# Gate and value of a gated MLP by Strassen's seven products, in three passes over the features

## The chip, the core and the metric

One NeuronCore of a Trainium2 chip runs the whole program in one launch. The metric is the device time of one execution in microseconds (us). Times of one kernel are medians over several runs; the profile is one profiled execution.

## The reference

An attention over chunks feeds two MLPs, all in float32 with 3072 tokens and a model width of 512. The change touches the second MLP alone:

```python
def _moe2_ref(x, w_gate, w_val, w_out):      # x 3072x512, w_gate, w_val 512x1536, w_out 1536x512
    g = x @ w_gate
    silu = g * (1.0 / (1.0 + np.exp(-g)))
    val = x @ w_val
    return (silu * val @ w_out).astype(np.float32)
```

Its input x is the output of the first MLP (width 2048, squared ReLU). The weights arrive as 64-bit floats and are turned into float32 on the chip.

## The kernel before, in words

Precision: every float32 operand of a large matmul is split into a rounded part `hi` and a residue `lo` (both float32r), and a product is three matmuls into one PSUM bank, hi*hi, hi*lo and lo*hi (`product`, L417 to 420). A weight tile and its rounding are made by `split` (L591): ScalarE or VectorE takes the magnitude of the upper words, VectorE bounds (L606), shifts (L610), sets sign and lower bits (L615, L622), one of the two rounds to `hi`, and VectorE subtracts (L632).

Staging: the first MLP goes over eight tiles of 384 tokens; each tile's output is stored to `y_dram`. The second MLP goes over the same eight tiles. For each tile t and each of the 12 feature tiles j of 128 features (a step), TensorE makes `gate` and `val` (`second_up`, L529: four blocks of k of 128, three matmuls of 384 columns each, so 12 and 12), ScalarE takes silu of gate (L542), VectorE multiplies by val (L546), one of the two rounds the product to `ghi`, VectorE makes the residue `glo` (L478), and in the step after TensorE adds three 128-token pieces of the down product, nine matmuls of 512 columns, to the accumulators `oacc` (`second_down`, L548). After twelve steps the accumulators are copied out (L558) and stored to `out`. All 36 weight tiles of the second MLP are converted once, in 18 pairs of 1 MB, and stay in SBUF; the memory for them comes from slots of `wp` (17, each held by one converted pair or one raw pair) that the first MLP's last tile gives back one by one, and two more (`EXTRA`).

Order: no engine chooses its work at run time. `Plan` (its `run`) is a list scheduler in the program: each piece of work has an engine, an assumed length, dependencies, and buffers as counted rooms (`get`, `put`) or rings (`take`, `give`). TensorE's order is the order in which pieces are added; the order on VectorE, ScalarE and SyncE (which issues all DMAs) is that in which the planner's clock would start them, the longest way to the end first. Each engine then runs its instructions in that order and waits on semaphores. `either` picks ScalarE or VectorE for a piece, by the list `MOVED`.

The step's order on TensorE in the second MLP stands in the loop at L861: `plan_up2` of a step, then `plan_down2` of the step before.

Of the kernel before, what the change touches and what calls it, by code (L numbers as in the profile page):

```python
# [14 lines left out]
ALU = mybir.AluOpType  # L15
# [118 lines left out]
def attention_and_two_mlps(  # L134
# [41 lines left out]
    N2 = 3 * M2 // 2  # L176
    EXTRA = 2
# [30 lines left out]
    part_dram = dram.tile([P, KD, T], F32, name="part_dram")  # L208

# [39 lines left out]
    def source2(i):  # L249
        j, n = divmod(i, 3)  # L250
        cols = slice(j * P, (j + 1) * P)
        return (w_gate[:, cols], w_val[:, cols], w_out2[cols, :])[n]

    def load_w2(p):
        raw2[p] = load_slot((source2(2 * p), source2(2 * p + 1)), f"second{p}")

    def weight2(j, n):
        p, h = divmod(3 * j + n, 2)
        w = w2[p]
        return w[:, 0, h * 512:(h + 1) * 512], w[:, 1, h * 512:(h + 1) * 512]  # L260
# [156 lines left out]
    def product(o, whi, wlo, xhi, xlo, first, last):  # L417
        nc.tensor.matmul(o, whi, xhi, start=first, stop=False)  # L418
        nc.tensor.matmul(o, whi, xlo, start=False, stop=False)  # L419
        nc.tensor.matmul(o, wlo, xhi, start=False, stop=last)  # L420
# [89 lines left out]
    yp = w2p = None  # L510
    y_f = {}

    def load_y(t, i):
        yf = yp.tile([P, T], F32, tag="yf", name=f"yf{t}_{i}")
        nc.sync.dma_start(out=yf, in_=y_dram[t][:, i])
        y_f[t, i] = yf

    def round_y(engine, t, i):
        if i == 0:
            y_t[t] = tuple(xp.tile([P, KD, T], F32R, tag=f"x{n}", name=f"y{n}{t}") for n in ("hi", "lo"))  # L520
        copy(engine, y_t[t][0][:, i], y_f[t, i])

    def residue_y(t, i):
        yhi, ylo = y_t[t]
        nc.vector.tensor_tensor(
            out=ylo[:, i], in0=y_f.pop((t, i)), in1=yhi[:, i].bitcast(F32), op=ALU.subtract
        )

    def second_up(t, j, n):  # L529
        yhi, ylo = y_t[t]  # L530
        pool, tag = ((ps_h, "h"), (ps_a, "a"))[n]
        o = pool.tile([P, 512], F32, tag=tag, name=("gate", "val")[n])[:, :T]
        whi, wlo = weight2(j, n)
        for kd in range(KD):
            c = slice(kd * P, (kd + 1) * P)
            product(o, whi[:, c], wlo[:, c], yhi[:, kd, :], ylo[:, kd, :], kd == 0, kd == KD - 1)
        g_t[t, j, n] = o

    def second_silu(t, j):
        r = gp.tile([P, T], F32, tag="r", name="sil")  # L540
        g_t[t, j] = r, None
        nc.scalar.activation(out=r, in_=g_t.pop((t, j, 0)), func=AF.Silu)  # L542

    def second_times(t, j):
        r, _ = g_t[t, j]
        nc.vector.tensor_tensor(out=r, in0=g_t.pop((t, j, 1)), in1=r, op=ALU.mult)  # L546

    def second_down(t, j, i):  # L548
        whi, wlo = weight2(j, 2)
        phi, plo = g_t[t, j]  # L550
        if j == 0:
            acc[t, i] = ps_acc.tile([P, 512], F32, tag=f"acc{i}", name=f"oacc{i}")
        c = slice(i * P, (i + 1) * P)
        product(acc[t, i][:, :DM], phi[:, c], plo[:, c], whi, wlo, j == 0, j == M2 - 1)

    o_t = {}

    def second_out(engine, t, i):  # L558
        o = o_t[t, i] = yp.tile([P, DM], F32, tag="o", name="o", bufs=2)
        copy(engine, o, acc[t, i][:, :DM])  # L560

    def second_store(t, i):
        r0 = t * T + i * P
        nc.sync.dma_start(out=out[r0:r0 + P, :], in_=o_t.pop((t, i)))
# [5 lines left out]
        dict(w=SLOTS - LENT, fly=2),  # L570
        dict(
            sc=LENT, f=2, own=1, q=2, k=2, v=3, kt=2, qt=1, at=1, x=2, r=3, ghi=2, glo=2, acc01=1,
            acc23=1, a=2, h=2, yf=3, o=2,
# [17 lines left out]
    def split(landed, raw, key, pool, name, done):  # L591
# [33 lines left out]

        def hi(engine):
            done[key] = pool().tile([P, 2, CH], F32R, tag="w", name=f"w_{name}")
            copy(engine, done[key][:, 0], held["f"].bitcast(F32))
# [13 lines left out]
        t = plan.add(DVE, 1.14, rest, [t], lag=0.5)  # L642
        t = either(f"h_{name}", {ACT: 0.95, DVE: 0.65}, hi, [t], lag=0.5)
        return plan.add(DVE, 1.14, lo, [t], put=["w"])
# [109 lines left out]
    y_parts = {}  # L754

    def open_second():
        nonlocal w2p, yp
        attn.close()
        w2p = ctx.enter_context(tc.tile_pool(name="w2p", bufs=EXTRA, reuse_waits="tile"))
        yp = ctx.enter_context(tc.tile_pool(name="yp", bufs=3, reuse_waits="tile"))  # L760

    def plan_w2(p):
        if p not in split2:
            landed = transfer(opened, lambda: load_w2(p), 2, 1024, ["w"] if p < EXTRA else ["w", "w"])
            split2[p] = split(landed, raw2, p, lambda: w2p if p < EXTRA else wp, f"second{p}", w2)
        return split2[p]

    def plan_y(t):
        y_parts[t] = []
        for i in range(KD):  # L770
            y = transfer([*opened, y_stored[t, i]], lambda i=i: load_y(t, i), 1, 192, take=["yf"])
            hi = either(f"z{t}_{i}", {ACT: 0.45, DVE: 0.35}, lambda e, i=i: round_y(e, t, i), [y, *y_parts[t][-1:]], take=["x"] if i == 0 else ())
            y_parts[t].append(plan.add(DVE, 0.48, lambda i=i: residue_y(t, i), [hi], give=["yf"]))

    def plan_up2(t, j):
        gate = plan.add(
            PE, 2.08, lambda: second_up(t, j, 0), [plan_w2(3 * j // 2), *y_parts[t]], take=["h"]
        )
        e = plan.add(ACT, 0.50, lambda: second_silu(t, j), [gate], take=["r"], give=["h"])
        val = plan.add(  # L780
            PE, 2.08, lambda: second_up(t, j, 1), [plan_w2((3 * j + 1) // 2)], take=["a"],
            give=["x"] if j == M2 - 1 else (),
        )
        e = plan.add(DVE, 0.57, lambda: second_times(t, j), [val, e], give=["a"])
        e = either(f"p{t}_{j}", {ACT: 0.43, DVE: 0.35}, lambda e: round_hi(e, t, j), [e], take=["ghi"])
        g_ready[t, j] = plan.add(DVE, 0.48, lambda: residue(DVE, t, j), [e], take=["glo"], give=["r"])

    def plan_down2(t, j):
        outs = []
        for i in range(NSUB):  # L790
            outs.append(plan.add(
                PE, 2.08 / NSUB, lambda i=i: second_down(t, j, i),
                [g_ready[t, j], plan_w2((3 * j + 2) // 2), *(acc_free[i:i + 1] if j == 0 else ())],
                give=["ghi", "glo"] if i == NSUB - 1 else (),
            ))
        if j == M2 - 1:
            for i in range(NSUB):
# [50 lines left out]
    for s in range(len(order) + 1):  # L848
        for half in range(2):
# [7 lines left out]
            if half and s > downs:  # L857
                plan_down1(*order[s - 1])
    opened.append(plan.add(SP, 0.1, open_second, [last_x[0]]))
    plan_y(0)  # L860
    for s in range(NB * M2 + 1):  # L861
        if s < NB * M2:
            t, j = divmod(s, M2)
# [45 lines left out]
```

## Time and profile before

| | |
|---|---|
| median of 3 runs | 1293.04 us (1291.48 to 1293.15) |
| profiled execution, first to last instruction (span) | 1292.1 us |
| TensorE matmul busy | 1261.9 us, 7776 matmuls |
| VectorE busy | 590.1 us |
| ScalarE busy | 504.4 us |
| mean granted TensorE clock | 0.996 |

The profile records one execution. PE is TensorE's matmul, PEld its weight load, DVE VectorE, ACT ScalarE, SPq the queue of DMAs that SyncE issues. Matmuls overlap in the pipeline and their ends are modelled, so how fast they follow each other is read from the start times, not from the durations. L542 is line 542 of the kernel. A row `a<-b` names what an instruction writes and reads.

### The profile page before, as it was taken

Reading aid. Unit: us, or ns where it says so; the run is one execution under the profiler, and the core shown is the slowest. Engines: PE = TensorE matmul, PEld = TensorE weight load, DVE = VectorE, ACT = ScalarE, POOL = GpSimd, SP = SyncE. Lnnn points to the kernel's source line nnn. Section 1 sums busy time; section 2 is a strip of 40 time slices with the busy share of each in tenths; the row PEclk is TensorE's granted clock in tenths of the full one; section 3 lists DMA queues with packets and bytes.
Section 4 is the critical chain, followed back from the end, with each engine's and each line's share of the span. In section 5 each row is a group of like instructions: output and inputs, shape, how many; then the busy total and the mean of one; then the engine's idle time right before and its main releaser. Section 6 shows DMA issues by size and latency. Waiting matters only on the chain.

```text
span 1292.1 us, 19275 instructions
## 1 busy us (share of the span) xinstructions
PE 1261.9 (98%) x7776; PEld 1200.1 (93%) x7776; DVE 590.1 (46%) x1406; ACT 504.4 (39%) x1248; POOL 0.7 (0%) x6
## 2 busy tenths in 40 slices
PE   5899999999999999999999999999999999999998
PEld 4788999999999999999999999999999999999997
DVE  6999765444444444453999841211212121121211
ACT  6976555545445454442565221211212121121111
POOL 0000000000000000000000000000000000000000
PEclk9899999999999999999999999999999999999999
DMA  9972232112121121110663210000101000000000
GB/s 191 263 211 97 74 83 70 39 38 62 32 62 38 39 62 32 48 48 13 214 226 123 89 51 1 25 25 1 50 1 49 1 28 22 1 31 1 25 1 25
DMA packets 131201, 80.42 MB, mean 62 GB/s; under 512 B 95144, under 2 KB 124328, under 8 KB 131112
## 3 DMA queue, kind: packets, MB, share of 16 engines
q1 hardware_dynamic: 131112, 79.19, 22.6%
q8 instruction: 61, 1.00, 0.3%
q14 instruction: 28, 0.23, 0.1%
HBM read 65.80 MB, written 13.37 MB: 61 GB/s over the span
## 4 chain that ended last, share of the span: by engine, by line
PE 92%; DVE 4%; ACT 3%; issue 1%; DMA 1%; SPq 0%; ACTq 0%; DVEq 0%
PE hp L418 7%; PE acc L419 6%; PE acc L418 6%; PE acc L420 6%; PE hp L419 6%; PE hp L420 6%; PE gate L420 5%; PE gate L418 5%; PE gate L419 5%; PE oacc L419 5%; PE oacc L420 5%; PE val L420 5%; PE val L418 5%; PE val L419 5%; PE oacc L418 5%; PE psS L329 3%
## 5 line engine op out<-in xcount | busy, mean ns | idle before, releaser
L546 DVE TENSOR_TENSOR sil<-val,sil 128x384 f32<-128x384 f32 x96 | 53.5, 557 | 362.0 <-PE val L420 362.0
L418 PE MATMUL hp<-xhi,w_first 128*128 128x384 f32 x512 | 177.7, 347 | 0.0
L419 PE MATMUL acc<-glo,w_first 128*128 128x384 f32 x512 | 171.6, 335 | 2.9 <-DVE glo L478 2.7
L418 PE MATMUL acc<-ghi,w_first 128*128 128x384 f32 x512 | 172.2, 336 | 1.6 <-ACT kq L212 1.3
L420 PE MATMUL acc<-ghi,w_first 128*128 128x384 f32 x512 | 171.4, 335 | 0.0
L419 PE MATMUL hp<-xlo,w_first 128*128 128x384 f32 x512 | 171.4, 335 | 0.0
L420 PE MATMUL hp<-xhi,w_first 128*128 128x384 f32 x512 | 171.3, 335 | 0.1
L542 ACT ACTIVATE sil<-gate 128x384 f32<-128x384 f32 x96 | 47.2, 492 | 265.8 <-PE gate L420 265.7
L420 PE MATMUL gate<-yhi,w_second 128*128 128x384 f32 x384 | 129.5, 337 | 0.0
L418 PE MATMUL gate<-yhi,w_second 128*128 128x384 f32 x384 | 129.3, 337 | 0.0
L419 PE MATMUL gate<-ylo,w_second 128*128 128x384 f32 x384 | 129.0, 336 | 0.0
L418 PE MATMUL val<-yhi,w_second 128*128 128x384 f32 x384 | 128.3, 334 | 0.0
L419 PE MATMUL val<-ylo,w_second 128*128 128x384 f32 x384 | 128.3, 334 | 0.0
L420 PE MATMUL val<-yhi,w_second 128*128 128x384 f32 x384 | 128.3, 334 | 0.0
L458 DVE SCALAR_TENSOR_TENSOR r<-r,s_sb 128x384 f32<-128x384 f32 x99 | 61.0, 616 | 141.1 <-ACT r L447 141.0
L420 PE MATMUL oacc<-w_second,glo 128*128 128x512 f32 x288 | 114.0, 396 | 0.0
L419 PE MATMUL oacc<-w_second,ghi 128*128 128x512 f32 x288 | 113.7, 395 | 0.0
L212 ACT ACTIVATE ghi<-sil 128x384 fp32r<-128x384 f32 x89 | 46.8, 526 | 167.4 <-DVE sil L546 166.6
L418 PE MATMUL oacc<-w_second,ghi 128*128 128x512 f32 x288 | 111.9, 389 | 0.0
L362 ACT ACTIVATE sc<-sc,mx 96x128 f32<-96x128 f32 x256 | 99.3, 392 | 22.6 <-DVE mx L357 22.4
L447 ACT ACTIVATE r<-hp 128x384 f32<-128x384 f32 x116 | 56.8, 489 | 124.9 <-PE hp L420 124.0
L419 PEld LDWEIGHTS acc<-glo,w_first 128*128 128x128 f32 x512 | 96.1, 188 | 4.2 <-DVE glo L478 3.6
(103 smaller groups left out, 2164.1 us busy)
## 6 DMA issues: line engine op xcount, KB each, us to landing
raw_first<-in_moe_w_in_dram SPq DMA_DIRECT2D x16, 512.0 KB
raw_first<-in_moe_w_out_dram SPq DMA_DIRECT2D x16, 512.0 KB
q<-in_q_dram SPq DMA_DIRECT2D x32, 192.0 KB
y_dram<-y SPq DMA_DIRECT2D x32, 192.0 KB
raw_second<-in_moe_w_gate_dram SPq DMA_DIRECT2D x12, 512.0 KB
raw_second<-in_moe_w_val_dram SPq DMA_DIRECT2D x12, 512.0 KB
yf<-y_dram SPq DMA_DIRECT2D x32, 192.0 KB
raw_second<-in_moe_w_out_dram SPq DMA_DIRECT2D x12, 512.0 KB
```

The costliest lines, as they stand in the source:

```text
L212: nc.scalar.activation(out=out, in_=in_, func=AF.Copy)
L329: nc.tensor.matmul(banks[e][:GQ, j * GK:(j + 1) * GK], qt[r, j, :], kt[r, j, :], start=True, stop=True)
L362: nc.scalar.activation(out=sc[:, h, :], in_=sc[:, h, :], func=AF.Exp, bias=mx[:, h:h + 1], scale=SCALE, accum_out=sm[:, h:h + 1],)
L418: nc.tensor.matmul(o, whi, xhi, start=first, stop=False)
L419: nc.tensor.matmul(o, whi, xlo, start=False, stop=False)
L420: nc.tensor.matmul(o, wlo, xhi, start=False, stop=last)
L447: nc.scalar.activation(out=r, in_=hp, func=AF.Relu)
L458: nc.vector.scalar_tensor_tensor(out=r, in0=r, scalar=s_sb[:, 0:1], in1=r, op0=ALU.mult, op1=ALU.mult)
L542: nc.scalar.activation(out=r, in_=g_t.pop((t, j, 0)), func=AF.Silu)
L546: nc.vector.tensor_tensor(out=r, in0=g_t.pop((t, j, 1)), in1=r, op=ALU.mult)
```

## The change

The second MLP is rearranged.

- Tiles of 512 tokens (`TS`), six of them (`NS`), each seen as two halves of 256 tokens (`TH`). The model width of 512 is seen as two halves of 256, and gate and value of one feature tile as the two halves of the output. On this 2x2 by 2x2 block product Strassen's scheme with seven products (Winograd's form) replaces the eight block products. A product has two k blocks of 128 and three split terms: six matmuls of 256 columns.
- The operand sums are made by VectorE: on the weights in `block_sum` (four sums of 256 columns for a feature tile, in the raw tile), on the tokens in `y_sums` (four of 512 elements). `hi` and `lo` of seven weight blocks take two slots for one feature tile; the down weights of two feature tiles take one slot.
- The output sums use two PSUM banks a step. Chain A takes product 1, is copied (`second_keep`, ScalarE), takes product 6 on top, is copied, takes 7, is copied, takes 4: that is the gate of the first half. Chain B takes 2 (VectorE adds the first copy: value of the first half), is begun anew with 5 (plus the third copy: gate of the second half) and takes 3 on top (plus the second copy: value of the second half).
- silu, product, rounding and residue are done by halves of 256 tokens. The down product takes four pieces of 128 tokens.
- Three passes (`PASSES`) of four feature tiles (`JP`), each over all six token tiles. The accumulators hold a pass; its sum is stored to `sum_dram`, loaded again in the next pass and added by VectorE. The seven token operands are made in the first pass, stored to `ops_dram` and loaded again in the other two.
- A pass's weights are loaded while the pass before runs, as slots come free (`put` at the last tile).

The core of the diff; the loop at its end sets TensorE's order:

```diff
+    TS = 512
+    TH = TS // 2
+    NS = NT // TS
+    PASSES = 3
+    JP = M2 // PASSES
...
+    def second_up(n, op):
+
+        h, s, j = step_of(n)
+        if op == 1:
+            st2[n] = {"A": ps_h.tile([P, 512], F32, tag="h", name="chain_a")[:, :TH]}
+        if op == 2:
+            st2[n]["B"] = ps_a.tile([P, 512], F32, tag="a", name="chain_b")[:, :TH]
+        o = st2[n]["A" if op in (1, 6, 7, 4) else "B"]
+        whi, wlo = w2[j]
+        at = {1: 1, 2: 2, 4: 0, 5: 3, 6: 4, 7: 5, 3: 6}[op]
+        xhi, xlo = y_t[h, s][1][op]
+        for k in range(2):
+            c = slice(at * 2 * P + k * P, at * 2 * P + (k + 1) * P)
+            first = k == 0 and op in (1, 2, 5)
+            last = k == 1
+            product(o, whi[:, c], wlo[:, c], xhi[:, k], xlo[:, k], first, last, op in (6, 7, 4, 3))
+
+    def second_keep(n, i):
+        st2[n][f"a{i}"] = t = sp.tile([P, TH], F32, tag=f"a{i}", name=f"kept{i}")
+        nc.scalar.activation(out=t, in_=st2[n]["A"], func=AF.Copy)
+
+    def second_add(n, what, i):
+        pool, tag, bufs = {"v1": (sp, "v1", 2), "v2": (sp, "v2", 1), "g2": (gp, "r", None)}[what]
+        st2[n][what] = t = pool.tile([P, TH], F32, tag=tag, name=what, **({"bufs": bufs} if bufs else {}))
+        nc.vector.tensor_tensor(out=t, in0=st2[n]["B"], in1=st2[n].pop(f"a{i}"), op=ALU.add)
...
+    def plan_up2(j):
+        if j not in split2:
+            landed = transfer([*opened, last_load[0]], lambda: load_up2(j), 2, 1024, ["w", "wt"] * 3, name=f"up{j}")
+            last_load[0] = issues[f"up{j}"]
+            split2[j] = split(landed, raw2, j, lambda: wp, f"up{j}", w2, ["w", "wt"], True)
+        return split2[j]
...
+    def plan_y_late(h, s):
+        key = h, s
+        if h:
+            for op in (7, 5, 4, 3):
+                y_ops[key, op] = transfer([kept[s, op]], lambda op=op: y_again(key, op), 1, 512, take=["z"])
+            return
...
+    def plan_product(n, op):
+        h, s, j = step_of(n)
+        key, d = (h, s), done2.setdefault(n, {})
+        before = {1: [], 2: [], 6: ["a1"], 7: ["a2"], 5: ["v1"], 4: ["a3"], 3: ["g2"]}[op]
+        last = j == (h + 1) * JP - 1
+        give = {6: ["x"], 7: ["z"], 5: ["z"], 4: ["z"], 3: ["z"]}.get(op, []) if last else []
+        p = plan.add(
+            PE, 0.70, lambda: second_up(n, op), [plan_up2(j), y_ops[key, op], *(d[b] for b in before)],
+            take={1: ["h"], 2: ["a"]}.get(op, []), give=give,
+            put=["w", "wt"] * 2 if op == 3 and s == NS - 1 else (),
         )
...
-    plan_y(0)
-    for s in range(NB * M2 + 1):
...
+    steps = PASSES * NS * JP
+    for n in range(-1, steps + 1):
+        if n + 1 < steps and (n + 1) % JP == 0:
+            plan_y(*step_of(n + 1)[:2])
+        for at, op, i in ((0, 6, None), (1, 1, None), (1, 2, None), (0, 7, 0), (0, 5, 1), (0, 4, 2), (0, None, 3), (0, 3, None)):
+            if op and 0 <= n + at < steps:
+                plan_product(n + at, op)
+            if i is not None and n > 0:
+                plan_part(n - 1, i)
+        if n + 1 < steps and (n + 1) % JP == 0:
+            plan_y_late(*step_of(n + 1)[:2])
```

## Rows read from the trace of the kernel before

**Rows 1.** The page: busy time of each engine, and the chain's shares.

```profile
PE 1261.9 (98%) x7776; PEld 1200.1 (93%) x7776; DVE 590.1 (46%) x1406; ACT 504.4 (39%) x1248; POOL 0.7 (0%) x6
...
PE 92%; DVE 4%; ACT 3%; issue 1%; DMA 1%; SPq 0%; ACTq 0%; DVEq 0%
```

**Rows 2.** Windows: length, busy by engine, clock, DMA share, GB/s.

```profile
618.50:685.20 66.70, 66.12 (x379) 65.28 (x378) 62.97 (x87) 40.45 (x60) 0.00 (x0) 1.00 0.63 207
685.20:1286.80 601.60, 601.60 (x3170) 563.73 (x3168) 173.42 (x286) 128.16 (x240) 0.00 (x0) 1.00 0.09 28
```

**Rows 3.** Waits of TensorE from 618.5 us on: total, times, longest.

```profile
PE acc L418 <- DVE ghi L471: 0.4, 1, 0.4
PE acc L419 <- DVE glo L480: 0.2, 1, 0.2
```

**Rows 4.** Timeline of the last step: start, duration, instruction, idle before it.

```profile
1280.43 0.33 PE L420 MATMUL gate<-yhi,w_second 128*128 128x384 f32 x1
1280.60 0.33 PE L418 MATMUL val<-yhi,w_second 128*128 128x384 f32 x1
...
1280.80 0.49 ACT L542 ACTIVATE sil<-gate 128x384 f32<-128x384 f32 x1 [3.00 <-PE gate L420]
...
1282.51 0.33 PE L420 MATMUL val<-yhi,w_second 128*128 128x384 f32 x1
1282.68 0.39 PE L418 MATMUL oacc<-w_second,ghi 128*128 128x512 f32 x1
...
1282.95 0.56 DVE L546 TENSOR_TENSOR sil<-val,sil 128x384 f32<-128x384 f32 x1 [4.56 <-PE val L420]
...
1286.58 0.39 PE L420 MATMUL oacc<-w_second,glo 128*128 128x512 f32 x1
1288.41 0.60 ACT L212 ACTIVATE o<-oacc 128x512 f32<-128x512 f32 x1 [2.17 <-DMA out_dram<-o]
```

**Rows 5.** Timeline of TensorE after a pause, first MLP.

```profile
316.51 0.19 PEld L418 LDWEIGHTS hp<-xhi,w_first 128*128 128x128 f32 x1
316.53 0.42 PE L418 MATMUL hp<-xhi,w_first 128*128 128x384 f32 x1
316.62 0.19 PEld L419 LDWEIGHTS hp<-xlo,w_first 128*128 128x128 f32 x1
...
316.79 0.34 PE L419 MATMUL hp<-xlo,w_first 128*128 128x384 f32 x1
316.79 0.19 PEld L420 LDWEIGHTS hp<-xhi,w_first 128*128 128x128 f32 x1
```

**Rows 6.** Timeline where a weight load waits for VectorE.

```profile
682.58 0.62 DVE L480 SCALAR_TENSOR_TENSOR glo<-r,b_sb,ghi 128x384 fp32r<-128x384 f32 x1
...
683.25 0.19 PEld L419 LDWEIGHTS acc<-glo,w_first 128*128 128x128 f32 x1 [0.47 <-DVE glo L480]
```

**Rows 7.** Groups by line and form: count, busy us, mean ns, idle before.

```profile
L546 DVE TENSOR_TENSOR sil<-val,sil 128x384 f32<-128x384 f32 x96 | 53.5, 557 | 362.0 <-PE val L420 362.0
L615 DVE SCALAR_TENSOR_TENSOR raw_second<-raw_second,t_second 128x1024 uint32<-128x1024 uint32 x18 | 22.0, 1223 | 0.3
L610 DVE TENSOR_SCALAR t_second<-t_second 128x1024 uint32<-128x1024 uint32 x18 | 12.5, 693 | 0.5
L214 DVE COPY o<-oacc 128x512 f32<-128x512 f32 x8 | 5.5, 691 | 7.4 <-PE oacc L420 7.4
...
L542 ACT ACTIVATE sil<-gate 128x384 f32<-128x384 f32 x96 | 47.2, 492 | 265.8 <-PE gate L420 265.7
L600 ACT ACTIVATE t_second<-raw_second 128x1024 f32<-128x1024 f32 x15 | 17.3, 1153 | 8.4 <-DMA raw_second<-in_moe_w_out_dram 4.6 <-DVE raw_second L615 2.5 <-DMA raw_second<-in_moe_w_gate_dram 1.2
```

**Rows 8.** The raw weights' tile: duration min, median, max, first and last start.

```profile
L615 DVE SCALAR_TENSOR_TENSOR raw_second<-raw_second,t_second x18: 1217/1221/1227, 618.6 to 746.9; 128x1024 uint32<-128x1024 uint32 x18
```

**Rows 9.** Groups of TensorE: the same split term for gate and value.

```profile
L418 PE MATMUL gate<-yhi,w_second 128*128 128x384 f32 x384 | 129.3, 337 | 0.0
...
L418 PE MATMUL val<-yhi,w_second 128*128 128x384 f32 x384 | 128.3, 334 | 0.0
```

More of the change, by code (lines that the diff above doesn't have):

```diff
@@ L509, in attention_and_two_mlps @@
     y_t = {}
-    yp = w2p = None
+    sp = None
     y_f = {}
[L513 to L524, printed above, removed]
+    o_t = {}
@@ L525, in residue_y, with second_lo @@
+    def second_lo(n, half):
+        st2[n][f"lo{half}"] = lo = gp.tile([P, TH], F32R, tag="glo", name="glo", bufs=2)
         nc.vector.tensor_tensor(
-            out=ylo[:, i], in0=y_f.pop((t, i)), in1=yhi[:, i].bitcast(F32), op=ALU.subtract
+            out=lo, in0=st2[n].pop(f"v{half + 1}"), in1=st2[n][f"hi{half}"].bitcast(F32), op=ALU.subtract
         )
[L529 to L564, printed above, removed]
+    def second_down(n, i):
+        h, s, j = step_of(n)
+        whi, wlo = (w2[f"down{j - j % 2}"][:, e, j % 2 * DM:(j % 2 + 1) * DM] for e in range(2))
+        half, c = divmod(i * P, TH)
+        phi, plo = (st2[n][f"{e}{half}"][:, c:c + P] for e in ("hi", "lo"))
+        if j == h * JP:
+            acc["second", i] = ps_acc.tile([P, 512], F32, tag=f"acc{i}", name=f"oacc{i}")
+        product(acc["second", i][:, :DM], phi, plo, whi, wlo, j == h * JP, j == (h + 1) * JP - 1)
+        if i == TS // P - 1:
+            st2.pop(n)
@@ new lines, in second_load, with second_out @@
+    def second_load(h, s):
+        o_t[s] = wp.tile([P, TS // P, DM], F32, tag="w", name="o")
+        nc.sync.dma_start(out=o_t[s], in_=sum_dram[h - 1][s])
+    def second_out(engine, h, s, i):
+        if h == 0 and i == 0:
+            o_t[s] = wp.tile([P, TS // P, DM], F32, tag="w", name="o")
+        o = o_t[s][:, i]
+        if h:
+            nc.vector.tensor_tensor(out=o, in0=acc["second", i][:, :DM], in1=o, op=ALU.add)
+        else:
+            copy(engine, o, acc["second", i][:, :DM])
@@ L567, in attention_and_two_mlps, with second_store @@
+    def second_store(h, s, i):
+        r0 = s * TS + i * P
+        nc.sync.dma_start(
+            out=out[r0:r0 + P, :] if h == PASSES - 1 else sum_dram[h][s][:, i], in_=o_t[s][:, i]
+        )
     ACT, DVE, PE, SP, MOVE = "ACT", "DVE", "PE", "SP", "MOVE"
@@ L589, in transfer, with split @@
         return plan.add(MOVE, kilobytes / rate, None, [issue], put=["fly"], lag=1.8, give=give)
-    def split(landed, raw, key, pool, name, done):
+    def split(landed, raw, key, pool, name, done, put=("w",), sums=False):
         held = {}
@@ L753, in attention_and_two_mlps @@
     opened = []
-    y_parts = {}
+    y_ops = {}
+    done2 = {}
+    last_load = [None]
     def open_second():
-        nonlocal w2p, yp
+        nonlocal sp
         attn.close()
[L759 to L766, printed above, removed]
@@ L788, in plan_down2 @@
[L788 to L797, printed above, removed]
-                e = either(f"o{t}_{i}", {DVE: 0.65, ACT: 0.6} if i % 2 else {ACT: 0.60, DVE: 0.65}, lambda e, i=i: second_out(e, t, i), [outs[i]], take=["o"])
-                acc_free[i:i + 1] = [e]
-                transfer([e], lambda i=i: second_store(t, i), 1, 256, give=["o"])
+        sp = ctx.enter_context(tc.tile_pool(name="sp", bufs=1, reuse_waits="tile"))
```

252 lines of the change are left out of this document (211 added, 41 removed).

## The prediction

> **What bounds the kernel now.** I read the summary and the chain of waits first, to see which engine carries the span. TensorE is busy 98% of it and holds 92% of the chain [rows 1]: what counts is how long the row of matmuls is and where it has holes. Next the windows: the second MLP runs from 685.20 to 1286.80 us, 601.6 us, TensorE busy in all of it at granted clock 1.00, that is at its 2.4 GHz level, VectorE in 173 us and ScalarE in 128 us of it, the DMA engines 9% [rows 2]. The waits of TensorE from the last tile of the first MLP on come to 0.6 us [rows 3]. So the second MLP is a gapless stream of matmuls; every other engine has room.
>
> Then the pace of that stream, from the timeline of the last step. Start to start, eleven intervals between the first and the last `val` matmul (1280.60 to 1282.51) make 0.1736 us for 384 columns; seventeen intervals between `oacc` matmuls (1282.68 to 1286.58) make 0.2294 us for 512 [rows 4]. That is 0.452 and 0.448 ns a column: no fixed part that I can see, so the time follows the columns. Check: 96 steps of 24 matmuls of 384 and 9 of 512 give 96 x (24 x 0.1736 + 9 x 0.2294) = 598.2 us against 601.6.
>
> **The change part by part.**
>
> *Columns of gate and value.* Before: 96 steps x 24 = 2304 matmuls of 384 columns, 884,736 columns. After: a step takes 512 tokens and one tile of 128 features, 6 x 12 = 72 steps, each seven products x 2 blocks of k x 3 split terms = 42 matmuls of 256 columns: 3024 matmuls, 774,144 columns. Removed: 110,592 columns x 0.452 ns = **50.0 us**. The down product has the same 864 matmuls of 512 columns.
>
> *Pace at 256 columns.* The trace of before has no matmul of this kind with 256 columns. By columns it takes 256 x 0.452 = 0.1157 us. Each matmul brings its own weight load (7776 of both [rows 1]). A record of a weight load lasts 0.19 us, longer than 0.1157, but what counts is how soon the next one may follow: after a pause, where no stream is in the way, two loads start at 316.51 and 316.62, 0.11 us apart, and only the next matmul, at 316.79, waits for the 384-column stream [rows 5]. So the lower end is 0.1157 (streaming), with the load at 0.11 just hidden, and the upper end is 0.1736, if a pair never goes faster than the ones we see in the stream. I take 0.1157, nearer to the 0.11 row, plus 1 ns: the `gate` matmuls run 3 ns longer in the mean than the `val` ones [rows 9], some jitter that I give a third of. 3024 x 1 ns = **+3 us**. At the upper end: 3024 x 0.058 = +175 us.
>
> A rule speaks against this part. What the row shows: the loads go out at the start of the matmul before [rows 5], and the pace at 384 columns is in proportion to that at 512 [rows 4], as if the load cost nothing. The Trainium skill ("TensorE: Matmul & The Clock Gate", section "Measured speedup vs the span model", its list of what overlaps) says that a weight load overlaps a matmul in flight only where the row groups differ; all loads here use all 128 rows. By that rule load and stream would add up. It is rival E below, and the pace at 384 columns speaks against it.
>
> *The two chains.* Product 1 is kept by ScalarE, product 6 goes on top of it in the same bank, is kept, then 7, kept, then 4; products 2, 5, 3 in the other bank. TensorE now waits within a step: 6 and 7 for ScalarE's copy of the bank, 5 and the next but one's 2 for VectorE's sum. The cost of one hand-over: from the start of the last matmul to ScalarE's start 0.37 us, to VectorE's 0.44 [rows 4], each 0.06 less at 256 columns. VectorE takes 0.557 for 384 and 1.223 for 1024 [rows 7], so 0.42 for 256; ScalarE by 0.492 and 1.153 [rows 7] 0.36. From VectorE's end (682.58 + 0.62) to the weight load that waited for it is 0.05 us [rows 6], and the load takes 0.11. Sum: by ScalarE 0.31 + 0.36 + 0.05 + 0.11 = 0.83 us, by VectorE 0.96. Cover: between 6 and 7 lie products 1 and 2 of the next step, with 6's own last matmul 13 x 0.1157 = 1.50 us; between 2 and 5 lie product 7 and one part of the down product, 7 x 0.1157 + 3 x 0.229 = 1.50 us; between 3 and the 2 of two steps later, products 6 and 1, again 1.50. So 0.5 to 0.7 us to spare; the other waits have more. Free otherwise: zero. Behind a waiting matmul stands all of TensorE.
>
> The spare time is gone where a long instruction sits on the engine: the weight conversion has pieces of 1.22 us on VectorE (L615) and 1.15 on ScalarE (L600) [rows 7]. A sum that becomes ready behind a fresh 1.22 us piece comes 0.7 us late; uniformly met, mean 0.2 us. There are 18 conversions, each spread over about 1.5 steps; with three tight waits a step and a third of them hitting: 18 x 1.5 x 3 x 0.33 x 0.2 = 5 us, of which the planner's order avoids some: **+4 us**. Ends: 0 and, if every tight wait there meets the full 0.7 us, 57.
>
> *Work of the other engines.* A step has on VectorE three sums, two products and two residues, 7 x 0.42 = 3.0 us, on ScalarE three copies, two silu, two roundings, 2.5 us, of a step's 42 x 0.1157 + 12 x 0.229 = 7.6 us. In the first pass the operands add 11 x 0.69 (512 columns [rows 7]) = 7.6 us of VectorE a tile, 2 us a step. Weight conversion: two of 0.69, two of 1.22, four block sums of 0.42, residues of 0.95 and 1.22, 7.7 us for each of twelve up pairs, 5 us for each of six down pairs. The cover holds except at the start.
>
> *The start.* Before, 18 conversions run from 618.6 to 746.9 [rows 8], with VectorE busy 62.97 of 66.7 us [rows 2], and TensorE hardly notices. After, the first load takes three slots at once; one is free, and the last tile gives one back with each step of 24 x 0.1736 = 4.2 us, the first after two, so the load goes out some 12 us into that tile and has landed some 6 us later. That leaves 48 us to 685, of which VectorE's first-MLP work (16 residues of 0.62 [rows 6] and some ten pieces like them in 66.7 us) takes a quarter: 36 us free, enough for the first operands (7.6), three up pairs (23) and a down pair (5). The fourth up pair, a down pair and the next operands, 20 us, fall into the first 30 us of the second MLP, of which the steps leave 60%, 18 us; and TensorE's fourth step needs up pair 3 after some 15 us, 9 us of VectorE. I take **+3 us** (0 to 10).
>
> *Transfers.* Passes two and three fetch 3.5 MB of operands and 1 MB of partial output a tile and store 1 MB, 5.5 MB in 30.5 us, 180 GB/s; in the window before 685 the queues move 207 GB/s at 63% of the engines [rows 2], so 330 at full share. The tight place is a tile's end: the operands of product 5 can be fetched only when its buffer's product 7 is done, and 1.5 MB of a later tile may go first. 2 MB at 330 GB/s are 6 us, plus some 2 to land (a 256 KB store holds a copy up for 2.17 [rows 4]), against twelve groups of 0.69 us, 8.3 us. Just covered: 0; uncovered, 2 us at each of 11 boundaries.
>
> *The end.* Last copy: before, the third output copy waits 2.17 us for a store [rows 4]; after, the tile has room for all four, about 2 us less. The last step has nothing between 6 and 7, and only two parts (1.5 us) under the last sum, product, rounding and residue (2.3 us): 1.5 us more. Net 0.
>
> Sum, against the profiled execution's span: 1292.1 - 50.0 + 3 + 4 + 3 + 0 = 1252.1 us. The median of the runs, 1293.04, is 0.9 above that span, so **1253 us**, own range 1242 to 1263.
>
> **The rivals.**
>
> *B, weight loads set the pace.* If the hand-over at the array leaves no overlap to spare, a pair takes the 0.11 load plus 10 to 18 ns: 0.120 to 0.128 us, +13 to +37 us on the 0.1157: 1262 to 1287. For it: 6 ns of slack is little. Against: rows 5.
>
> *C, the waits are dearer.* VectorE saturated in the first pass, 2 us at each tile boundary (+22), or up to half of the full collisions (+25 over my 4): in sum +12 to +35, 1265 to 1288. For it: VectorE goes from 173 us to some 390 in this part (72 x 3.0 + 45 operands + 90 weights + 40 output). Against: the order of the queues puts what TensorE waits for first.
>
> *D, slower: a matmul with its own weight load has a floor of 0.1736 us whatever its columns.* Then 720 more matmuls cost instead of fewer columns saving: +175, 1253 - 3 + 175 = 1425 us. It decides from 0.1157 + (50 - 7)/3024 = 0.130 us a matmul on: above it the change loses. For it: every load in the stream is recorded at 0.19 us. Against: rows 5, and the proportion between 384 and 512.
>
> *E, slower: load and stream in sequence.* 0.1157 + 0.11 = 0.226 us a matmul, 3024 x 0.11 = +333: 1583 us. Against: at 384 columns it would be 0.28 where 0.1736 stands. This is what the rule of the Trainium skill named above would make of it.
>
> That it does not do what it says would show as a count other than 3024; from the loops I see none.
>
> **How the numbers follow.** A 0.64, B 0.14, C 0.15, D 0.06, E 0.01. Range: A's own, up to most of B and C, with a little below for terms that come out at nothing: 1240 to 1277. A measurement of this kernel tells 0.2% (2.6 us) from no change. A, and nearly all of B and C, are faster: 0.90; the top of B and C within: 0.03; D and E slower: 0.07.
>
> **What would show it.** The start-to-start time of products of 256 columns: 0.116 to 0.118 right, 0.12 to 0.13 B, 0.17 D. The second MLP's TensorE stretch: about 560 us. TensorE's waits on ScalarE's copies and VectorE's sums: under 5 us in total, all beside weight conversions; waits for DMA at every tile boundary, a sixth of a pass, would be C. Wrong altogether if the steps of the second pass, far from any conversion, take clearly more than 7.7 us.

## The result and the profile after

The changed kernel takes 1259.46 us (median; 1258.74 to 1260.1) against 1293.1 us before (1291.48 to 1294.65): ratio 0.9739, 95% interval 0.9725 to 0.9753. Forecast: 1253 us, range 1240 to 1277. The direction, the bound and the saving by columns held; the pace at 256 columns did not, and the time is 6.5 us above the forecast.

The page of the changed kernel, busy time and the chain's shares:

```profile
PE 1225.2 (97%) x8496; PEld 1162.8 (92%) x8496; DVE 761.3 (61%) x1846; ACT 625.9 (50%) x1596; POOL 0.7 (0%) x6
...
PE 89%; DVE 6%; ACT 2%; DMA 1%; issue 1%; SPq 0%; DVEq 0%; ACTq 0%
```

720 more matmuls than in [rows 1], as the loops say (3024 for 2304), with 37 us less busy time. TensorE is still the bound; VectorE does 171 us more beside it.

Its windows (length, busy by engine in the order PE, PEld, DVE, ACT, POOL, granted clock, DMA share, GB/s): a stretch of the first MLP, the first MLP's last tile, the second MLP, and 200 us out of its middle:

```profile
82.00:88.00 6.00, 6.00 (x31) 5.78 (x28) 5.93 (x8) 2.70 (x4) 0.00 (x0) 0.52 0.62 172
618.50:689.30 70.80, 68.00 (x389) 67.06 (x388) 56.92 (x91) 42.33 (x68) 0.00 (x0) 1.00 0.52 182
689.30:1253.40 564.10, 562.24 (x3890) 523.85 (x3888) 351.41 (x725) 249.04 (x583) 0.00 (x0) 1.00 0.54 195
1000.00:1200.00 200.00, 200.00 (x1389) 186.78 (x1388) 113.69 (x239) 77.99 (x191) 0.00 (x0) 1.00 0.58 214
```

Against [rows 2] the second MLP is 564.1 us long instead of 601.6 and begins 4.1 us later. A step in the middle has 54 matmuls: 54 x 200 / 1389 = 7.78 us, without a hole.

Waits of TensorE from 618.5 us to the end (total, times, longest), to be held against [rows 3]:

```profile
PE acc L423 <- DVE glo L482: 1.8, 1, 1.8
PE chain_b L422 <- DVE g L615: 0.9, 1, 0.9
PE acc L422 <- DVE y L224: 0.8, 1, 0.8
PE chain_a L422 <- ACT kept L610: 0.8, 2, 0.5
PE acc L423 <- DVE glo L484: 0.2, 1, 0.2
```

The rows with `acc` belong to the first MLP's last tiles; the second MLP waits 1.7 us by this view, for no DMA.

The timeline of a product chain in the middle, the one pair without cover in the last step, and the end (start, duration, instruction):

```profile
1001.75 0.28 PE L422 MATMUL chain_a<-yhi,hi_up 128*128 128x256 f32 x1
1001.87 0.28 PE L423 MATMUL chain_a<-ylo,hi_up 128*128 128x256 f32 x1
...
1003.79 0.28 PE L424 MATMUL chain_b<-yhi,lo_up 128*128 128x256 f32 x1
...
1243.94 0.28 PE L424 MATMUL chain_a<-yhi,lo_up 128*128 128x256 f32 x1
1244.74 0.39 PE L422 MATMUL chain_a<-y,hi_up 128*128 128x256 f32 x1 [0.52 <-ACT kept L610]
...
1252.14 0.50 PE L422 MATMUL oacc<-w_down,ghi 128*128 128x512 f32 x1
...
1253.40 0.40 PE L424 MATMUL oacc<-w_down,glo 128*128 128x512 f32 x1
```

From the first to the last of 18 matmuls are 17 intervals, 2.04 us: **0.120 us each** where the forecast had 0.1167. By the forecast's own sign (0.12 to 0.13 B) that is rival B. From 1243.94 to 1244.74, 0.80 us, is one hand-over by ScalarE.

Where the difference of the spans comes from, with sums of start-to-start times (before, after):

| part | before | after | difference | forecast |
|---|---|---|---|---|
| products, holes left out | 401.8 | 360.8 (0.1193 each) | -41.0 | -47.0 |
| down product, holes left out | 199.5 | 200.1 | +0.6 | 0 |
| start: first product, holes of the first steps | 685.30 | 689.35, and 1.6 of holes | +5.7 | +3 |
| waits in the steps beside conversions | 0 | 0.35 | +0.35 | +4 |
| end: last step's holes 1.2, last matmul to end 5.52 to 4.07 | | | -0.3 | 0 |
| span | 1292.1 | 1257.5 | -34.6 | -40.0 |

The remaining 1.1 us of the 6.5 lie outside the span: the profiled execution of the change took 1259.23 us, 1.7 more than its span, where the forecast had set a median 0.9 above the span.

### The profile page after: what moved, and what is told of

Read it like the earlier page. It is cut to its first block, busy times and chain, and to the rows that moved or that the text cites. A ratio compares the mean times of both kernels' runs of the same rounds, so it can differ in the third digit from the quotient of the medians.

```text
span 1257.5 us, 22202 instructions
## 1 busy us (share of the span) xinstructions
PE 1225.2 (97%) x8496; PEld 1162.8 (92%) x8496; DVE 761.3 (61%) x1846; ACT 625.9 (50%) x1596; POOL 0.7 (0%) x6
## 4 chain that ended last, share of the span: by engine, by line
PE 89%; DVE 6%; ACT 2%; DMA 1%; issue 1%; SPq 0%; DVEq 0%; ACTq 0%
PE hp L422 7%; PE acc L423 6%; PE acc L422 6%; PE acc L424 6%; PE hp L423 6%; PE hp L424 6%; PE chain_a L422 5%; PE chain_a L423 5%; PE chain_a L424 5%; PE oacc L423 5%; PE oacc L422 5%; PE oacc L424 5%; PE chain_b L423 4%; PE chain_b L422 4%; PE chain_b L424 4%; PE psS L333 3%
## 5 line engine op out<-in xcount | busy, mean ns | idle before, releaser
L422 PE MATMUL hp<-xhi,w_first 128*128 128x384 f32 x512 | 177.9, 347 | 0.0
L422 PE MATMUL acc<-ghi,w_first 128*128 128x384 f32 x512 | 173.0, 338 | 2.1 <-ACT kq L222 1.3
L610 ACT ACTIVATE kept<-chain_a 128x256 f32<-128x256 f32 x216 | 83.0, 385 | 159.5 <-PE chain_a L424 132.2
L422 PE MATMUL oacc<-w_down,ghi 128*128 128x512 f32 x288 | 114.1, 396 | 0.1
L423 PE MATMUL oacc<-w_down,ghi 128*128 128x512 f32 x288 | 114.1, 396 | 0.0
L424 PE MATMUL oacc<-w_down,glo 128*128 128x512 f32 x288 | 112.0, 389 | 0.0
L484 DVE SCALAR_TENSOR_TENSOR glo<-r,b_sb,ghi 128x384 fp32r<-128x384 f32 x99 | 61.1, 617 | 68.5 <-ACT ghi L473 68.3
L422 PEld LDWEIGHTS acc<-ghi,w_first 128*128 128x128 f32 x512 | 96.6, 189 | 3.4 <-ACT kq L222 1.5
L422 PEld LDWEIGHTS hp<-xhi,w_first 128*128 128x128 f32 x512 | 96.4, 188 | 3.0
L423 PEld LDWEIGHTS hp<-xlo,w_first 128*128 128x128 f32 x512 | 96.5, 188 | 0.3 <-DVE xlo L415 0.3
L424 PEld LDWEIGHTS acc<-ghi,w_first 128*128 128x128 f32 x512 | 96.7, 189 | 0.0
L424 PEld LDWEIGHTS hp<-xhi,w_first 128*128 128x128 f32 x512 | 96.2, 188 | 0.0
L627 DVE TENSOR_TENSOR v<-v,g 128x256 f32<-128x256 f32 x144 | 60.9, 423 | 56.5 <-ACT g L623 54.6
L473 ACT ACTIVATE ghi<-r,b_sb 128x384 fp32r<-128x384 f32 x95 | 58.3, 614 | 52.6 <-DVE r L462 51.5
```

The lines of the kernel that those rows point to most:

```text
L422: nc.tensor.matmul(o, whi, xhi, start=first, stop=False, skip_group_check=onto)
L423: nc.tensor.matmul(o, whi, xlo, start=False, stop=False, skip_group_check=onto)
L424: nc.tensor.matmul(o, wlo, xhi, start=False, stop=last, skip_group_check=onto)
L473: nc.scalar.activation(out=hi, in_=r, func=AF.Identity, bias=bias)
L484: nc.vector.scalar_tensor_tensor(out=lo, in0=r, scalar=bias, in1=hi.bitcast(F32), op0=ALU.add, op1=ALU.subtract)
L610: nc.scalar.activation(out=t, in_=st2[n]["A"], func=AF.Copy)
```

## The experiments

**The stream by itself.** A kernel with nothing but runs of 48 matmuls in the pattern of `product` (`n` columns against `m` weight columns, each run into one bank, float32r); it computes nothing of the reference.

```diff
+    for name, n, m in STREAMS:
+        for r in range(REPS):
+            a = slice((r % 2) * P, (r % 2) * P + m)
+            nc.tensor.matmul(acc, whi[:, a], xhi[:, :n], ...)
+            nc.tensor.matmul(acc, whi[:, a], xlo[:, :n], ...)
+            nc.tensor.matmul(acc, wlo[:, a], xhi[:, :n], ...)
```

> Streams of 48 matmuls each by themselves, nothing else running: N columns streamed by 512, 384, 320, 288, 256, 240, 224, 192 with weights of 128 columns, then some of them with 96 or 64 weight columns. The kernel computes nothing of the reference. Theory W (the weight load sets the pace at 256: a load starts with the stream of the matmul before and needs 0.108 us, some 12 ns more go into the hand-over): 512 and 384 columns at 0.231 and 0.173 us, 320 and 288 at 0.145 and 0.130 (0.452 ns a column), 256 at 0.120 instead of 0.1157, and a floor of 0.120 at 240, 224 and 192; with 64 weight columns 256 columns at 0.1157 or less and 192 at 0.087. Rival S (the stream itself costs 0.120 at 256, a fixed part of some 4 to 10 ns, whatever the weights): 256 columns at 0.120 with 64 and with 128 weight columns alike, and 192 at about 0.091 with both. Rival I (in the kernel VectorE, ScalarE or DMA disturb the stream): 256 columns at 0.1157 here, where nothing else runs.

Measured, mean start to start in us:

| columns | 512 | 384 | 320 | 288 | 256 | 240 | 224 | 192 |
|---|---|---|---|---|---|---|---|---|
| 128 weight columns | 0.2267 | 0.1739 | 0.1465 | 0.1318 | 0.1199 | 0.1120 | 0.1115 | 0.1113 |
| 64 weight columns | 0.2300 | 0.1733 | | | 0.1135 | | 0.1031 | 0.0886 |

and 0.1163 for 256 columns against 96 weight columns. The trace shows each stream's every third matmul (duration min/median/max, first and last start):

```profile
L45 PE MATMUL fulle<-xhi,whi x16: 280/283/283, 61.5 to 66.9; 128*128 128x256 f32 x16
...
L45 PE MATMUL fullh<-xhi,whi x16: 258/275/276, 78.0 to 83.0; 128*128 128x192 f32 x16
...
L45 PE MATMUL slimd<-xhi,whi x16: 275/276/279, 108.2 to 113.4; 128*64 128x256 f32 x16
```

Between first and last start lie 45 intervals: 5.4 / 45 = 0.120 for `fulle` (256 columns), 5.0 / 45 = 0.111 for `fullh` (192), 5.2 / 45 = 0.116 for `slimd` (256, half the weight columns; the more exact sum gives 0.1135). So the 0.12 is TensorE's own: no other engine runs beside the streams (ScalarE copies a bank after each). Two limits show: with whole weights nothing goes below 0.111 (the load), and 256 columns with half the weights take 0.1135. Where both are near each other a pair takes 0.120, more than either. Both readings put ahead of the run missed: theory W had a floor of 0.120 at 192 to 240 columns (0.111 to 0.112 came), rival S 0.120 with 64 weight columns too (0.1135 came).

The Trainium skill ("TensorE: Matmul & The Clock Gate", section "LDWEIGHTS (loading the stationary operand)") puts a load at its columns over 1.2 GHz, an estimate of 107 ns for 128; the floor of 0.1113 us agrees within 5 ns. Its rule behind rival E, that a load overlaps a matmul in flight only with other row groups, stands in the section "The mechanism" (the forecast names the section after it). It is contradicted: all loads here use all rows, and 384 columns go at 0.1739 us with whole and at 0.1733 us with half the weight columns, so the load adds nothing there.

**The cover taken away.** Product 7 directly behind product 6.

```diff
-((0, 6, None), (1, 1, None), (1, 2, None), (0, 7, 0), (0, 5, 1), ...
+((0, 6, None), (0, 7, None), (1, 1, None), (1, 2, 0), (0, 5, 1), ...
```

> Product 7 moved to stand right behind product 6, so that TensorE has nothing between them while ScalarE copies the bank. Theory (hand-over of 0.31 + 0.36 + 0.05 + 0.11 = 0.83 us from the start of 6's last matmul, hidden by the two products between): a hole of 0.83 - 0.12 = 0.7 us in each of 72 steps, +50 us, 1309 us; in the kernel as changed the one step that has nothing between them, the last, shows 0.80 us from start to start. Rival (most of the hand-over is hidden in the array's own pipeline, or the other waits of the step take over the time): holes under 0.3 us, under 1282 us.

Measured: 1319.72 us, 60 more than the change; the second MLP lasts 624.2 us. TensorE's waits:

```profile
PE chain_a L422 <- ACT kept L610: 41.3, 73, 1.7
```

One wait a step. Start to start the hole is 0.803 us and the matmul behind it starts 0.224 later; less two matmuls at pace that is 0.785 us a step, 56.5 us over 72; most of what is left of the 60 are a few longer holes. The hand-over was put at 0.83. So the order of the products hides what it was said to hide, and that is the price of one hand-over without it.

**The start: a load held back.** In the changed kernel the second token tile's load is free to go while the first MLP still runs, and VectorE does its sums before work that TensorE waits for:

```profile
632.29 0.69 DVE L543 TENSOR_TENSOR tsum<-yf 128x512 f32<-128x512 f32 x1 [3.01 <-DMA yf<-y_dram]
633.02 0.69 DVE L543 TENSOR_TENSOR tsum<-yf,tsum 128x512 f32<-128x512 f32 x1
633.63 0.68 DVE L543 TENSOR_TENSOR yf<-yf 128x512 f32<-128x512 f32 x1
634.23 0.55 DVE L482 TENSOR_TENSOR glo<-r,ghi 128x384 fp32r<-128x384 f32 x1
...
634.84 0.45 PE L423 MATMUL acc<-glo,w_first 128*128 128x384 f32 x1 [1.81 <-DVE glo L482]
```

This is the 1.8 us row of the waits: VectorE itself had waited 3.01 us for `yf` at the head of its queue, and the residue `glo` stood behind the sums. The experiment lets that load start only when the last tile's fifth `g_ready` is there:

```diff
+        held = [g_ready[NB - 1, 4]] if s == 1 else []
-        y = transfer([*opened, *stored], lambda: load_y(key), 2, 1024, ["w"], take=["yq"])
+        y = transfer([*opened, *stored, *held], lambda: load_y(key), 2, 1024, ["w"], take=["yq"])
```

> The load of the second token tile's operands waits until the first MLP's last tile has made its fifth hidden tile, so that VectorE's first sum of it isn't queued ahead of its transfer. Theory Q (VectorE stood 3.0 us at that sum, waiting for a load behind 3.6 MB of stores, and a residue of the first MLP queued behind it kept TensorE 1.8 us): that wait goes, 1.5 to 3 us less, 1257 us. Rival (the sums only move to where VectorE is full, at the start of the second MLP): no change or up to 3 us more.

Measured: 1254.85 us (1254.47 to 1255.51), ratio to before 0.970 (0.9686 to 0.9715); the second MLP begins at 684.70. The gain of 4.6 us is more than the wait. Both kernels were therefore run again on one chip.

> The changed kernel once more, beside the one with the late load on the same chip. The half-clock stretches in the first 100 us differ from one execution to the next (two more in its profile than before, worth 1.8 us). Theory (chance): the median is again 1258 to 1260. Rival (they belong to the kernel): the same, but then the late load, which has the same first 500 us, would lose 3 us less against it than the 4.6 seen.

> The late load once more, on the same chip: 1254 to 1256 if its gain of 4.6 us stands, of which 2.6 us lie in the first MLP's last tiles by the trace; 1256 to 1258 if 1.8 of the 4.6 was chance at the start.

Measured: the change 1258.26 us (ratio 0.9722, 0.9708 to 0.9736), the later load 1255.86 (0.9704, 0.969 to 0.9718): 2.4 us, both inside what was expected. The window from 618.50 to 640.00 us of the change's first profile, of its repeat, and of the repeated later load:

```profile
618.50:640.00 21.50, 18.87 (x108) 18.23 (x106) 14.97 (x27) 6.05 (x13) 0.00 (x0) 1.00 0.88 316
```

```profile
618.50:640.00 21.50, 18.64 (x97) 18.00 (x96) 12.33 (x22) 4.61 (x9) 0.00 (x0) 0.92 0.90 318
```

```profile
618.50:640.00 21.50, 20.69 (x120) 20.37 (x119) 15.41 (x27) 7.77 (x14) 0.00 (x0) 1.00 0.87 305
```

Against the first profile the later load lets 12 matmuls more into the same time at the same clock, 12 x 0.174 = 2.1 us: the wait. Against the repeat it is 23 more, 4.0 us. There the wait is 2.05 us long and the granted clock falls behind it to its 1.2 GHz level, from 633.25 to some 636.5:

```profile
632.43 0.44 PE L423 MATMUL acc<-glo,w_first 128*128 128x384 f32 x1 [2.05 <-DVE glo L482]
...
633.55 0.52 PE L422 MATMUL acc<-ghi,w_first 128*128 128x384 f32 x1
633.87 0.52 PE L423 MATMUL acc<-glo,w_first 128*128 128x384 f32 x1
```

These matmuls start 0.32 us apart instead of 0.174. Of the six profiles of kernels that have this wait (1.8 to 2.2 us in each: the change, its repeat and the runs on the cover, the half weights, the transfers and the conversions) five show the stretch, the first profile of the change alone does not; no profile of the later load has it. So the wait mostly costs a second time, by the clock, which its row of 1.8 us does not show; the two together are the 4.0 us. The rest moves between executions: the change has medians of 1259.46 and 1258.26, the later load of 1254.85 and 1255.86. It is the fastest version that computes the whole result, by about as much as a measurement can tell.

**Strassen undone, the passes kept.** Tiles of 512 tokens and three passes as in the change, but gate and value by 12 matmuls of 512 columns each; no operand sums, no chains.

```diff
+        for k, y in enumerate((1, 2, 6, 7)):
+            c = slice((op == "V") * 512 + k * P, (op == "V") * 512 + (k + 1) * P)
+            xhi, xlo = (e.rearrange("p a t -> p (a t)") for e in y_t[h, s][1][y])
+            product(o, w[:, 0, c], w[:, 1, c], xhi, xlo, k == 0, k == KD - 1)
```

> Strassen undone, the three passes kept: gate and value by twelve matmuls of 512 columns each, four operand blocks instead of seven, partial output through DRAM as in the change. Theory (the gain is the columns alone, the passes cost and bring nothing but the start): 72 x 36 x 0.2312 = 599 us for the second MLP against 601 before, the start late by up to 3 us: 1290 to 1297 us, about as before. Rival P (the passes themselves bring something, as fewer weight conversions ahead of the second MLP, or cost something, by transfers): more than 6 us away from the kernel before, on either side.

Measured: 1285.44 us (1284.39 to 1286.54), ratio 0.9934 (0.9917 to 0.995). The expectation failed: the passes and the wider tiles, without Strassen, bring 7.7 us.

```profile
692.60:1280.00 587.40, 587.40 (x2594) 486.48 (x2592) 209.93 (x421) 142.66 (x335) 0.00 (x0) 1.00 0.39 136
```

The stretch is 587.4 us, not some 599, and full; it starts 7.3 us later than before, of which 3.7 are one wait (`PE acc L422 <- DVE y L224`). With the columns of before, 1728 matmuls take 391.7 us, 0.2267 each, instead of 401.8, and the 864 of the down product 195.6 instead of 199.5. The expectation had used 0.231, read from before's stream where 384 and 512 columns alternate. Against this kernel Strassen brings 26.0 us of the median, 26.6 of the span: 28.1 in the products (391.7 to 363.6, holes among them), 3.3 by an earlier start, less 4.9 that the down product pays.

**Mixed widths by themselves.** Streams like those of the first experiment (nothing of the reference), two widths in turn, a bank for each.

```diff
+    ("only", 1, ((512, 128, 96),)),
+    ("before", 6, ((384, 128, 24), (512, 128, 9))),
+    ("after", 12, ((256, 128, 18), (512, 128, 3))),
+    ("pairs", 48, ((256, 128, 1), (512, 128, 1))),
+    ("threes", 12, ((256, 128, 6), (384, 128, 6))),
+    ("slim", 12, ((256, 64, 18), (512, 128, 3))),
```

> Streams by themselves again, nothing of the reference computed, now with changing widths: 512 columns only; 24 of 384 and 9 of 512 in turn as in the kernel before; 18 of 256 and 3 of 512 as in the change; one of 256 and one of 512 in turn; six of 256 and six of 384; 18 of 256 with 64 weight columns and 3 of 512 with 128; 512 only. Theory M (a stream of mixed widths is slower than its parts, with nothing else running): 512 columns at 0.2267 in the first and last stream and at 0.230 to 0.232 in the mixed ones, 256 at 0.1195 to 0.120, with 64 weight columns at 0.114 to 0.115. Rival K (what makes 0.231 of 0.2267 lies in the kernel, other engines or the memory's addresses): 0.2267 in all streams.

Measured: 512 alone 0.2267; beside 384 columns 0.2312 (384: 0.1744); beside 256 columns 0.2325 (256: 0.1194); in turn one by one 0.2301 and 0.1167; beside 256 columns with 64 weight columns 0.2323 and 0.1139; 256 and 384 in sixes 0.1182 and 0.1743. In the timeline of the stream like the change's:

```profile
101.26 0.28 PE L51 MATMUL after_x<-xhi,wlo 128*128 128x256 f32 x1
101.38 0.40 PE L51 MATMUL after_y<-xhi,whi 128*128 128x512 f32 x1
101.61 0.40 PE L51 MATMUL after_y<-xlo,whi 128*128 128x512 f32 x1
101.85 0.39 PE L51 MATMUL after_y<-xhi,wlo 128*128 128x512 f32 x1
102.07 0.28 PE L51 MATMUL after_x<-xhi,whi 128*128 128x256 f32 x1
```

The three of 512 take 0.69 us from 101.38 to 102.07 (the mean over the stream is 3 x 0.2325 = 0.70), where three in a row of their own take 0.68. So the mixing itself slows the wide ones, with no other engine at work; why is open. It is not the only thing that does: in the first experiment 512 columns against 64 weight columns take 0.2300 in a row of their own.

**Half the weight columns in the kernel.** 39 of a step's 42 products load 64 weight columns; the lower 64 rows of those products are left out.

```diff
+            few, h = slice(c.start, c.start + P // 2), o[:P // 2]
+            wide = (o, whi[:, c]) if first else (h, whi[:, few])
```

> In 39 of a step's 42 product matmuls the weights have 64 columns instead of 128, so that a weight load takes half as long while 256 columns are streamed as before; the products' lower 64 rows are left out or incomplete. Theory (in the kernel as in the stream measured by itself, the weight load is what lifts the pace at 256 columns from 0.1135 to 0.120): 39 x 72 x 0.006 = 17 us less, about 1242 us, pace 0.113 to 0.114. Rival (in the kernel something else sets 0.1195, as the changing banks or the other engines): no change, 1257 to 1261 us, pace 0.119 to 0.120.

Measured: 1243.72 us in two runs, the second MLP 549.07 us, 15.0 less than the change. The same 200 us window:

```profile
1000.00:1200.00 200.00, 200.00 (x1431) 183.58 (x1428) 114.07 (x242) 79.51 (x196) 0.00 (x0) 1.00 0.56 204
```

54 x 200 / 1431 = 7.55 us a step against 7.78. Holes left out, a product matmul takes 0.1143 us in the mean instead of 0.1193 (0.113 to 0.114 were expected, and 17 us). With half the weight columns the stream comes back to near its own pace, inside the full kernel too. The edit halves the load and the rows written alike; that the load is what counts is read from the first experiment, where half the weight columns change nothing at 384 columns (0.1739 to 0.1733) and lower the time at 192 (0.1113 to 0.0886).

**Twice the transfers.** Every reloaded operand is also stored once more, 44 MB in all.

```diff
+                transfer([y_ops[key, op]], lambda op=op: y_more(key, op), 1, 512)
```

> In passes two and three each reloaded operand is also stored once more to DRAM, 44 MB more traffic, some 120 GB/s on top of 195. Theory (transfers are hidden with room: a tile's boundary has 8.3 us for 2 MB at 330 GB/s): within 1.5 us of the changed kernel, 1258 to 1261 us, no wait of TensorE for a DMA. Rival C (just covered): 2 us or more at each of 11 boundaries, 1280 us or more.

Measured: 1259.95 us (1258.86 to 1261.05), the second MLP 564.58 us against 564.05.

```profile
1000.00:1200.00 200.00, 199.91 (x1385) 186.44 (x1384) 113.22 (x238) 77.61 (x189) 0.00 (x0) 1.00 0.86 329
```

The DMA share rises from 0.58 to 0.86 and TensorE stays full. The transfers are hidden with room; the part of rival C that waits at tile boundaries is out.

**The conversions first.** The planner takes the second MLP's weight conversions ahead of all else on VectorE and ScalarE: a test of the price of collisions.

```diff
+            plan.ahead = 1e6
-                    ready[t.engine].append((-t.way, n))
+                    ready[t.engine].append((-t.way - t.ahead, n))
```

> The pieces of the second MLP's weight conversions go ahead of everything else in the planner's order, so that the 1.2 us pieces on VectorE and ScalarE lie where they fall and not where the planner found room. Theory (0.5 to 0.7 us to spare at three waits a step; uniformly met, 5 us over 18 conversions and up to 57): waits of TensorE for copies and sums in the second MLP grow from 3 us to 8 or more, 1264 us or more. Rival (the spare time absorbs the pieces in any order): under 1262 us.

Measured: 1312.32 us in two runs, ratio to before 1.0137 (1.0117 to 1.0158), 53 more than the change: slower than the kernel before. TensorE's waits, the windows up to the first product and from there to the last matmul, and a stretch of VectorE's timeline:

```profile
PE chain_b L423 <- DVE v L616: 19.0, 6, 10.0
PE acc L424 <- DVE glo L483: 13.6, 3, 7.7
```

```profile
618.50:708.20 89.70, 73.98 (x377) 71.68 (x376) 63.30 (x96) 44.32 (x67) 0.00 (x0) 0.89 0.39 137
708.20:1306.60 598.40, 573.29 (x3888) 530.85 (x3888) 349.35 (x716) 245.85 (x579) 0.00 (x0) 0.98 0.51 184
```

```profile
902.91 0.69 DVE L710 TENSOR_SCALAR t_up<-t_up 128x1024 f32<-128x1024 f32 x1
...
904.36 1.23 DVE L719 SCALAR_TENSOR_TENSOR raw_up<-raw_up,t_up 128x1024 uint32<-128x1024 uint32 x1
...
912.70 1.22 DVE L758 TENSOR_TENSOR lo_up<-raw_up,hi_up 128x1024 fp32r<-128x1024 f32 x1
913.84 0.42 DVE L616 TENSOR_TENSOR v<-chain_b,kept 128x256 f32<-128x256 f32 x1
```

One whole conversion and most of another run in a row and the sum `v` stands at their end: 10 us at once, not single pieces of 1.22 us met by chance as the forecast's model had it. Not all of the 53 us are collisions in the second MLP: it begins 18.8 us later (708.19), as the 13.6 us of waits for `glo` lie in the first MLP's last tile, where the granted clock is 0.89; and it is 34.4 us longer (598.4 against 564.05). Of these 34.4 the waits are 23 (24.7 against 1.7), and some 8 are matmuls at half clock behind the long waits (granted clock 0.98 over the stretch). The direction was expected, the size not. It shows that the collisions are small in the change because of the planner's order, not because VectorE has room.

**The planner's lengths as measured.** The later load, and the assumed lengths of the new pieces set to what the trace gives (the edit in short form).

```diff
-DVE, 0.61   (y_sums, y_lo)      +DVE, 0.69
-DVE, 0.36   (block_sum and others)   +DVE, 0.43 or 0.44
-{ACT: 0.57, DVE: 0.35}          +{ACT: 0.63, DVE: 0.45}
```

> The late load of the second tile's operands, and besides the planner's lengths for the new VectorE and ScalarE pieces set to what the trace shows (operand sums and residues 0.69 instead of 0.61, block sums, products and residues 0.43 to 0.44 instead of 0.36, operand roundings 0.63 and 0.45). Theory (the remaining waits at the start, 0.8 for an output copy of the first MLP, 0.2 and 0.9 in the second MLP's first steps, come from an order made with lengths that are too short): 1 to 2 us less than with the late load alone, 1253 us. Rival (the order hardly changes, or trades one wait for another): 1254 to 1256 us.

Measured: 1255.41 us (1254.23 to 1256.41), ratio 0.9697 (0.9681 to 0.9713): the same as the later load alone. Waits were traded (1.0 us of `acc` for `ghi` and 0.5 for the sum `v` came, the 0.8 for `y` and 0.7 of the 0.9 for `g` went); the second MLP starts at 685.4 and lasts 564.3 us. No gain.

## Why the prediction was right, and what missed

- **The bound and the columns: right.** The stretch followed the matmul stream, and 110,592 columns fewer paid. The products gave 41.0 us of the forecast 47.0: at the forecast's 0.1157 they would have given 51.9 (401.8 less 3024 x 0.1157, as before's pace is 0.1744 and not 0.1736), and the pace took 10.9 of it.
- **"Pace at 256 columns", +3 us: the term that was mis-sized.** "with the load at 0.11 just hidden" is what failed. Load and stream each came out as put (floor 0.1113, stream 0.1135 with half the weights), but a pair in which both are nearly equal takes 0.1193 in the kernel. Over the 0.1157 that is 3.6 ns x 3024 = 11 us, not 3. This is the lower edge of rival B (0.120), which the forecast kept apart with 0.14; the streams of the first experiment show the pace, and the half weights take it away again. Nor is it rival B as it was argued: its 10 to 18 ns on top of the load came from no row, and at 192 to 224 columns a pair takes 0.111, the load with nothing on top. The jitter seen in [rows 9] was not its measure.
- **The pace read from [rows 4]: right for this stream, its reading too simple.** 0.2294 for 512 columns came from 17 intervals of one step; over the whole of before it is 199.5 / 864 = 0.231, and 0.1744 for 384. "No fixed part that I can see" compared a 384 and a 512 from the same mixed stream; alone, 512 columns take 0.2267.
- **The two chains: right.** Hand-over by ScalarE forecast 0.83 us, measured 0.80 in the last step and 0.785 net a step when the cover was taken away. By [rows 3]'s view TensorE waits 1.7 us in the second MLP, under the 5 forecast; but not "all beside weight conversions": the last step and the first ones hold most of it. By start-to-start times the holes are 3.15 us.
- **Collisions, +4: 0.35.** The ends given (0 and 57) contain what happened. In another order the same pieces cost 34 us inside the second MLP, but by whole conversions in a row and the clock behind the waits, not by the model of single pieces. Taking chance where a planner has arranged the order was the fault.
- **The start, +3 (0 to 10): 5.7.** The first product came 4.05 us later in this profile: about 2 us by the load named above, and 1.8 us have no part of the change in them. From 82 to 88 us TensorE ran at granted clock 0.52, about its 1.2 GHz level, after short transposes and a wait of 1.13 us for ScalarE; the profile of the change's repeat has no such stretch there; it has the one behind the wait at 632.43 instead, and its first product at 688.49. The other 1.6 us are holes in the first steps, the longest a wait for VectorE's sum `g`.
- **What was luck.** Two misses on the other side hid 5.5 us of the pace: before's true pace (1.9) and the collisions (3.65). Without them the time would have been some 1265 us: inside the range, but outside the forecast's "own range" of 1242 to 1263 for its first reading.
- **Transfers 0: right**, with twice the stores as well. **The end 0: right** (-0.3): the tail after the last matmul became 1.5 us shorter, the last step's holes took 1.2.
- **Rivals.** D (a floor of 0.1736) and E (load and stream in sequence, 0.226) fall with the 0.120. Of C nothing is left in this order of the queues: no wait of TensorE for a DMA, 0.35 us beside conversions, 1.6 in the first steps.

What stays open: why two nearly equal limits cost 6 ns more than the larger, and why mixed widths cost the wide ones 5 ns.

## What to carry to other kernels

Fewer columns pay in full only while the moving columns stay clear of the weight load: here, with 128 weight columns, 288 to 384 went by their columns (0.453 to 0.458 ns each), 256 paid some 6% (0.120 for 0.1135), and below 240 nothing more was gained. An algebraic saving should be held against the same tiling without it (here 26 of the 34 us were Strassen's, the rest the tiling's uniform width). A dependent chain in PSUM is cheap where about 0.8 us of other products lie between its links, and that cover, like the order on VectorE's queue, is what to protect when such a kernel is edited.

## What was not expected of the hardware

- 256 columns: 0.1135 us a matmul with 64 weight columns, 0.1163 with 96, 0.120 with 128, while 192 to 224 columns with 128 weight columns take 0.111.
- 512 columns: 0.2267 us in a row of their own (0.2300 with 64 weight columns), 0.230 to 0.2325 beside narrower ones; and 256 columns in turn with 512 one by one 0.1167, faster than in a row (0.120).
- The first 100 us, the same program in all of them, were granted 0.97 of the clock before, 0.93 in the change and its repeat, 0.97 and 0.91 in the two profiles of the later load. In the change one such stretch cost 1.8 us; what it makes of the whole is not settled, for the profile with 0.91 has the shortest span of these (1252.6 us).
- A wait of TensorE of 1.8 to 2.2 us after a full stream: in five of six profiles the granted clock fell to half behind it; in the repeat of the change that cost some 1.7 us beside the wait.
